# Fused attention and mixture of experts on one core: SyncE's queue in the source's order, weight quarters held for a GpSimd write, and a gather that the weights wait for

## The chip, the cores and the metric

One core of one Trainium2 chip runs the whole program in one launch. The metric is device microseconds of that core, the median of the runs. TensorE (PE) multiplies; VectorE (DVE), ScalarE (ACT) and GpSimd (POOL) do the elementwise work; SyncE (SP) issues nearly all the DMAs.

## The reference

The first half is attention with eight global keys and a causal window of 96, on (4 batches, 8 heads, 768 positions, 64 wide):

```python
keep = is_global | is_local
scores = np.where(keep, scale * q @ k.T - slopes * dist, -1e9)
a = exp(scores - max); a = a / (a.sum(-1) + 1e-9)
x = (a @ v)                       # 3072 tokens of 512
```

The second half routes each token to the best of 8 experts by `x @ w_gate`. An expert keeps its 80 tokens of the largest gate value and computes `gate * (relu(x @ w1[e]) @ w2[e])`, with w1[e] 512 by 1024 and w2[e] 1024 by 512. All other rows of the (3072, 512) output are zero.

## The kernel before

All data are fp32. **Attention** goes through 24 blocks of 128 positions in the order TURN, in two rounds of four heads each, so that round u treats block u // 2 (`for u in range(nu - 1)`, L344, with the last round written out in DRAIN). A round is a pipeline over engines: PE makes the scores of round u (L156), DVE adds the position table and takes the minimum (L167), ACT takes the exponential (L171), GpSimd divides by the sum for round u - 1 (`norm`, L184), PE transposes the probabilities of round u - 2 (L201 to L214), ACT and DVE copy them to SBUF (L218, L224), and PE multiplies those of round u - 3 by the values (`weigh`, L246, L256). Every fourth round also computes router logits. The first compare of DVE (L167) marks where a round stands.

Blocks are loaded into four buffers each of q, va and vb (`load_blk`, L383, called in even rounds for the block two ahead, that is four rounds ahead). The keys of the next batch come in three pieces (`keys`, L348). The first 16 of 64 **weight quarters** of 512 KB are loaded during attention (`ahead`, L350), and the whole output is cleared by twelve DMAs of zeros of 512 KB (`wipe`, L352). PE, DVE, ACT and GpSimd run in the order of the source (`manual_schedule(engines=ORDERED)`); SyncE is not among them, so a planner chooses the order in which the DMAs stand in its queue.

Attention's result is kept transposed. It must lie in DRAM by rows (`x_dram`) for a later gather. For 8 of the 24 blocks (INSIDE) the turning back is done within the rounds from 29 (FROM) on, beside the probabilities' transposes (L214), half a block per round, and stored from the same copy (L227). Three more blocks are turned in the drain (`x`, `y`, L101 to L107), and 13 in `select` (`rows`, L109 to L122): PE transposes two blocks, ACT copies them to one of three pairs of buffers, SyncE stores them. ROWS gives how many such pairs stand at each step of the search.

**The drain** (DRAIN, L52) is a hand-written order of steps; `r` is one step of the routing of a group of blocks, `c` one of the last group's choice, `x` the turning of a block. **`select`** searches the gate value at which each expert has 80 tokens, then compares ranks with slot numbers (`at`, L688, four compares of 480 elements) and multiplies (L692) to get the index table `gi`. **`experts`** gathers each expert's 80 rows by an indirect DMA on GpSimd's queue (`gather`, L724), fills PE's wait with idle products (`busy`, 11 and 7 of them, L542), transposes the first expert's tokens (`tokens`, L756) and then runs both layers of each expert as three fp32r products per tile (L762), with the weights split into two parts by ACT (L740) and DVE (L743, a few on GpSimd). A split frees the buffer for the next of the remaining 48 quarters (L85).

Of the kernel before, what the change touches and what calls it, by code (L numbers as in the profile page):

```python
# [10 lines left out]
F32 = mybir.dt.float32  # L11
# [11 lines left out]
P = 128  # L23
# [21 lines left out]
MASK = -8.0e9 * 64  # L45

EARLY = "k12 q1 v0 k23 v1 q2 k36 w0 v2"
WIPE = 34
FROM, INSIDE = 29, 8


DRAIN = (  # L52
    "r a1 t45 w44 r r r n47 r r a2 t46 r r r r w45 r r r "
    "t47 w46 r b1 w47 r r b2 c1 c c2 c r r x x x c3 y y y r r c c r"
)
NORM = (("V", slice(2, 4)), ("G", slice(0, 2)))
ROWS = (2, 2, 1, 0, 2)
WARM = (0, 0, 0, 0, 0, 11)
SPLIT = (4, 4, 4)
FAR = 1.0e6  # L60
# [4 lines left out]
def fast_path(tc, a, out, cst, x_dram, inp):  # L65
# [4 lines left out]
    with ExitStack() as ctx:  # L70
# [7 lines left out]

        def load_w():

            for k, e, c in QUARTERS:
                t = wp.tile([P, DF], F32, tag="w", name=f"w{k}_{e}_{c}")
                raw[k, e, c] = t
                src = (a["w1"] if k == 1 else a["w2"])[e].rearrange("(c p) f -> p c f", p=P)
                yield nc.sync.dma_start(out=t.rearrange("p (c f) -> p c f", c=k), in_=src[:, k * c:k * c + k])  # L85

# [5 lines left out]
                )  # L92

        room = inp.kt[1].rearrange("p q k -> p (q k)")[:, :6 * DM].rearrange("p (n d) -> p n d", n=6)
        due = [INSIDE]
        halves = [slice(64 * i, 64 * i + 64) for i in range(2)]

        def turned(t, xp):
# [10 lines left out]
        def rows(t, n, xp):  # L109

            xp = xp.rearrange("p i (n c) -> p i n c", n=2)
            for j in range(n):
                ut = uts.pop(t + j)
                for pr in range(NP):
                    for i, h in enumerate(halves):
                        T.transpose(out=xp[:, i, j, 64 * pr:64 * pr + 64], in_=ut[h, pr, :], identity=ident[h, h])
            j = 2 * (t // 2 % 3)
            x = room[:, j:j + n].rearrange("p n (i c) -> p n i c", i=2)
            A.copy(out=x, in_=xp[:, :, :n].rearrange("p i n c -> p n i c"))
            for j in range(n):  # L120
                nc.sync.dma_start(
                    out=x_dram[TURN[t + j] * P:(TURN[t + j] + 1) * P, :], in_=x[:, j].rearrange("p i c -> p (i c)"))  # L122

        with tc.tile_pool(name="at_sb", bufs=2) as sp, tc.tile_pool(name="ps_a", bufs=1, space=PSUM) as psa, ExitStack() as pctx:
# [215 lines left out]
            weights = load_w()  # L340
            ahead = islice(weights, NW)
            wipe = clear()
            sp_ctx.enter_context(tc.manual_schedule(engines=ORDERED))
            for u in range(nu - 1):  # L344
                if u % (2 * NB) == 1 and u // 2 // NB + 1 < B:
                    keys = inp.keys(u // 2 // NB + 1)
                if keys and u % 2 == 0:
                    keys = keys if next(keys, END) is not END else None  # L348
                elif u > 1:
                    next(ahead, None)  # L350
                if u >= WIPE:
                    next(wipe, None)  # L352
                if u == 0:
                    next(cst["first"])
                begin(u)
                scores(u)
                if u % 4 == 0 and 8 <= u:
                    logits2(u // 2 - 4, 2)
                if u == 0:
                    window = window_tables(nc, cst)  # L360
                if 2 <= u:
                    copied(u - 2)
                if u == 0:
                    for _ in cst["first"]:
                        pass
                if u < 2:
                    for _ in islice(window, 3 - u):
                        pass
                if u == 1:
                    for z in pwz:  # L370
                        G.memset(z[:, 4 * WH:], 0.0)
                    G.memset(cst["zero"], 0.0)
                if u == 2:
                    for _ in window:
                        pass
                if u > 2:
                    for _ in range(3):
                        next(late, None)
                if u % 4 == 3 and 7 <= u:
                    logits1((u - 7) // 2, 2)  # L380
                if 3 <= u:
                    weigh(u - 3)
                if u % 2 == 0 and 3 <= u // 2 + 2 < NT:  # L383
                    inp.load_blk(u // 2 + 2)
                routes(3)
            u = nu - 1
            begin(u)
# [272 lines left out]
def select(tc, cst, lps, gs1, rows, due, w, early):  # L660

    nc = tc.nc
    V, G, T = nc.vector, nc.gpsimd, nc.tensor
    gi, si, gs, bx = cst["gi"], cst["si"], cst["gs"], cst["bx"]

    with tc.tile_pool(name="sel2", bufs=2) as s2, tc.tile_pool(name="ps_s", bufs=1, space=PSUM) as pp, \
            tc.tile_pool(name="ps_r", bufs=2, space=PSUM) as pr, tc.manual_schedule(engines=ORDERED):
        slot = s2.tile([P, NT], BF16, name="slot", bufs=1)

        def more(n):  # L670
            for _ in range(min(n, (NT - due[0] + 1) // 2)):
                t = due[0]
                due[0] = min(NT, t + 2)
                rows(t, due[0] - t, pr.tile([P, 2, 512], F32, tag="xp", name=f"xp{t}"))

        for i, own in enumerate(search(nc, s2, s2, pp, cst, gs1, slot)):
            if i == len(ROWS):
                break
            more(ROWS[i])
            for j in range(len(early)):  # L680
                if SPLIT[j] == i:
                    nc.scalar.copy(out=early[j], in_=w[1, 0, j])
            busy(nc, cst, lps, WARM[i])
        more(NT)
        ix = pp.tile([CAP, 6, E], F32, tag="cnt", name="ix")
        for i in range(4):
            at = s2.tile([P, CAP, NT // 4], BF16, tag="at", bufs=4, name=f"at{i}")
            V.tensor_tensor(  # L688
                out=at, in0=cst["svx"], in1=slot[:, 6 * i:6 * i + 6].unsqueeze(1).broadcast_to([P, CAP, 6]), op=ALU.is_equal)
            for j in range(6):  # L690
                t = 6 * i + j
                T.matmul(ix.rearrange("p k e -> p (k e)"), at[:, :, j], bx[:, t].rearrange("p k e -> p (k e)"), start=t == 0, stop=t == NT - 1)  # L692
        busy(nc, cst, lps, WARM[-1])
        with nc.allow_low_precision(reason="integers"):
            V.tensor_reduce(out=gi, in_=ix[:, :2, :].rearrange("p k e -> p e k"), axis=AX.X, op=ALU.add)
        xs = s2.tile([CAP, 6, E], F32, name="xsel")
        V.tensor_copy(out=xs, in_=ix)
        tok = s2.tile([CAP, E], F32, name="tok")
        V.tensor_tensor(out=tok, in0=xs[:, 0, :], in1=xs[:, 1, :], op=ALU.add)
        V.tensor_tensor(out=gs, in0=xs[:, 3, :], in1=xs[:, 4, :], op=ALU.add)  # L700
        V.tensor_tensor(out=gs, in0=gs, in1=xs[:, 5, :], op=ALU.add)
        vm = s2.tile([CAP, E], F32, name="vm")
        V.tensor_scalar(out=vm, in0=xs[:, 2, :], scalar1=-BIG, scalar2=BIG, op0=ALU.mult, op1=ALU.add)
        V.tensor_tensor(out=si, in0=tok, in1=vm, op=ALU.add)
        full = s2.tile([1, E], F32, name="full")
        V.tensor_tensor(out=full, in0=own, in1=cst["cap8"][:1], op=ALU.is_equal)
        V.tensor_reduce(out=cst["sure"], in_=full, axis=AX.X, op=ALU.min)


def experts(tc, out, cst, x_dram, inp, raw, weights, lps, early, hip):  # L710
# [5 lines left out]
    with tc.tile_pool(name="ffn", bufs=2) as fp, tc.tile_pool(name="hl", bufs=NLO) as hl, \  # L716
# [97 lines left out]
                ready[k, e, c] = split(raw.pop((k, e, c)), DF, f"w{k}_{e}_{c}")  # L814
                next(weights, None)

        with tc.manual_schedule(engines=ORDERED):
            for e in range(E):
                gather(e)
            prepare(2)  # L820
            busy(nc, cst, lps, 7)
            tokens(0)
            prepare(2)
            for e in range(E + 1):
# [277 lines left out]
def late_constants(nc, a, c, fast=True):  # L1102
# [37 lines left out]
    yield iota(nc, sv, 1, 1)  # L1140
    yield iota(nc, s1, 2, 1)
    yield V.scalar_tensor_tensor(out=s1, in0=sv, scalar=cap, in1=s1, op0=ALU.is_le, op1=ALU.mult)
    yield V.tensor_scalar(out=c["svx"], in0=s1.unsqueeze(2).broadcast_to([P, CAP, NT // 4]), scalar1=-1.0, scalar2=None, op0=ALU.add)


def late_tiles(c):
    for n, k in (("pref", E), ("kval", 31), ("kval1", P - 1), ("tval", NT), ("pval", E), ("cap8", E), ("capm", E), ("pick", E), ("gate", NT)):
        c.tile(n, [P, k])
    for n, k in (("sval", CAP), ("sval1", CAP), ("ones", P), ("ones32", P), ("ones16", P), ("tri", P), ("keep", 2 * E * (NT + 1)), ("mz", 2 * E * (NT + 1))):
        c.tile(n, [P, k], BF16)  # L1150
    c.tile("svx", [P, CAP, NT // 4], BF16)
    c.tile("bx", [P, NT, 6, E], BF16)
    c.tile("gs1", [P, E], BF16)
    c.tile("left", [P, 2, NT])
# [13 lines left out]
class Inputs:  # L1168
# [4 lines left out]
    def __init__(self, nc, a, ip):  # L1173
        self.nc, self.a, self.ip = nc, a, ip
        self.kts, self.blk = {}, {}
        self.q = [ip.tile([P, NP * P], F32, name=f"q{i}") for i in range(self.NQ)]
        self.kt = [ip.tile([P, NP, NB * KB], F32, name=f"kt{i}") for i in range(2)]
        self.va, self.vb = ([ip.tile([P, H * D], F32, name=f"{n}{i}") for i in range(self.NQ)] for n in ("va", "vb"))
        for g in range(2):
            self.load_k(0, slice(2 * g, 2 * g + 2), 0, KB)  # L1180
            self.load_q(0, slice(2 * g * P, 2 * g * P + 2 * P))
# [113 lines left out]
```

## Time and profile before

| | us |
|---|---|
| median of 3 runs | 282.01 |
| lowest and highest | 280.45, 283.68 |
| the profiled execution | 283.87 |
| its span, first to last instruction | 282.2 |
| mean granted TensorE clock, share of full | 0.94 |

The profiled execution lies 1.9 us above the median; 1.7 us of its time lie outside the span. Times in the rows count from the start of the span. Attention takes the span up to about 150 us, the drain and `select` up to 171, the gather up to 179, the experts up to 278, and the last scatter the rest. A row of a timeline gives the start, the duration of the merged instructions, engine, line, what is written from what, and their number; in brackets the idle time of the engine before it and what ended it.

### The profile page before, as it was taken

How to read it: one execution, taken by the hardware profiler on the slowest of the kernel's cores; microseconds unless marked ns; L12 is line 12 of the kernel's file. 1: busy time of each engine (PE TensorE's matmuls, PEld its weight loads, DVE VectorE, ACT ScalarE, POOL GpSimd, SP SyncE). 2: the span in 40 equal slices, each digit the busy share in tenths (PEclk: the TensorE clock that was granted, in tenths of full speed). 3: DMA queues.
4: the chain of work that ended last, by engine and by line, in shares of the span. 5: the costliest groups of instructions: out<-in, count | busy, mean ns of one | idle time of the engine just before them, and what ended most of it. 6: DMA issues, size and time to landing. Idle time of an engine off the chain costs nothing. (4 is left out here: it accounts for less than half of the span.)

```text
span 282.2 us, 9562 instructions
## 1 busy us (share of the span) xinstructions
PE 254.0 (90%) x3565; PEld 185.8 (66%) x3565; DVE 216.4 (77%) x784; ACT 206.1 (73%) x582; POOL 123.9 (44%) x171
## 2 busy tenths in 40 slices
PE   2699799969899999999999799699999999999992
PEld 2477577657667778778776685366666666656661
DVE  3967557766757898688977675579999999998960
ACT  2778667965748888898886554478798977979740
POOL 5356543533326534653544403750717346152421
PEclk9999979997959999999999857799999999999997
DMA  6999999999999996564210485999999999992001
GB/s 181 307 282 384 300 314 340 325 299 317 331 397 358 388 372 215 160 211 156 94 42 20 147 313 193 259 319 362 313 300 390 380 343 394 339 354 79 23 28 29
DMA packets 40875, 73.06 MB, mean 259 GB/s; under 512 B 3413, under 2 KB 14549, under 8 KB 40821
## 3 DMA queue, kind: packets, MB, share of 16 engines
q1 hardware_dynamic: 39652, 69.74, 73.8%
q0 software_dynamic: 1024, 2.62, 3.2%
q8 instruction: 30, 0.49, 0.8%
q14 instruction: 25, 0.20, 0.2%
q10 hardware_dynamic: 144, 0.00, 0.0%
HBM read 58.46 MB, written 13.89 MB: 256 GB/s over the span
## 5 line engine op out<-in xcount | busy, mean ns | idle before, releaser
L171 ACT ACTIVATE pwz<-ts,nm 128x168 f32<-128x168 f32 (+1 forms) x192 | 80.8, 422 | 34.3 <-DVE nm L167 32.9
L184 POOL TENSOR_TENSOR pwz<-pwz,z 128x672 f32<-128x672 f32 (+2 forms) x48 | 60.4, 1257 | 75.3 <-ACT pwz L171 66.2
L167 DVE CUSTOM_DVE_ANT_0 ts<-sc,tab 128x168 f32<-128x168 f32 (+1 forms) x192 | 53.2, 315 | 30.0 <-PE sc L156 29.7
L156 PE MATMUL sc<-kt,q 64*64 64x104 f32 (+3 forms) x1088 | 45.8, 290 | 11.8 <-issue 6.0
L156 PEld LDWEIGHTS sc<-kt,q 64*64 64x64 f32 x1088 | 36.1, 146 | 14.6 <-issue 13.6
L743 POOL TENSOR_TENSOR w_3l<-w,w_3h 128x1024 fp32r<-128x1024 f32 x7 | 23.7, 3382 | 43.9 <-issue 26.3
L171 ACT ACTIVATION_READ_ACCUMULATOR pwz<-ts,nm 128x1 f32 x192 | 36.2, 188 | 0.0
L246 PE MATMUL u<-ta,va 104*64 104x128 f32 (+1 forms) x384 | 33.6, 299 | 0.4 <-ACT kt L271 0.4
L743 DVE TENSOR_TENSOR w_0l<-w,w_0h 128x1024 fp32r<-128x1024 f32 x15 | 28.3, 1890 | 3.0 <-ACT w_0h L740 3.0
L256 PE MATMUL u<-ta,vb 64*64 64x64 f32 x640 | 28.6, 231 | 0.0
L256 PEld LDWEIGHTS u<-ta,vb 64*64 64x64 f32 x640 | 22.9, 140 | 7.3 <-issue 6.3
L201 PE MATMUL tp<-ident,pwz 64*128 64x64 f32 x384 | 23.9, 246 | 4.2 <-POOL pwz L184 3.4
L246 PEld LDWEIGHTS u<-ta,va 104*64 104x64 f32 (+1 forms) x384 | 21.2, 143 | 9.7 <-issue 6.1
L224 DVE COPY ta<-tp 128x384 f32<-128x384 f32 (+2 forms) x48 | 27.5, 574 | 0.0
L201 PEld LDWEIGHTS tp<-ident,pwz 64*128 64x128 f32 x384 | 16.9, 147 | 12.4 <-POOL pwz L184 7.4
L218 ACT COPY ta<-tp 128x384 f32<-128x384 f32 (+2 forms) x48 | 22.8, 475 | 0.8 <-ACT pwz L171 0.8
L743 DVE TENSOR_TENSOR w_2l<-w,w_2h 128x1024 fp32r<-128x1024 f32 x15 | 19.8, 1320 | 0.5 <-ACT w_2h L740 0.5
L805 POOL DMA_INDIRECT out_dram<-vb,si x8 | 12.7, 1590 | 12.9 <-ACT vb L804 12.0
L743 DVE TENSOR_TENSOR w_1l<-w,w_1h 128x1024 fp32r<-128x1024 f32 x15 | 18.2, 1211 | 0.0
L740 ACT CAST w_2h<-w 128x1024 fp32r<-128x1024 f32 x15 | 15.9, 1058 | 1.2 <-PE hp L762 1.2
L740 ACT CAST w_3h<-w 128x1024 fp32r<-128x1024 f32 x16 | 16.7, 1046 | 0.0
L740 ACT CAST w_1h<-w 128x1024 fp32r<-128x1024 f32 x15 | 15.7, 1050 | 0.5 <-PE hp L762 0.5
(405 smaller groups left out, 519.7 us busy)
## 6 DMA issues: line engine op xcount, KB each, us to landing
w<-in_w_dram SPq DMA_DIRECT2D x64, 512.0 KB
out_dram<-zero SPq DMA_DIRECT2D x12, 512.0 KB
q<-in_q_dram SPq DMA_DIRECT2D x23, 256.0 KB
vb<-in_vb_dram SPq DMA_DIRECT2D x20, 256.0 KB
va<-in_va_dram SPq DMA_DIRECT2D x20, 208.0 KB
x_dram<-kt SPq DMA_DIRECT2D x13, 256.0 KB
kt<-in_kT_dram SPq DMA_DIRECT2D x4, 816.0 KB
x_dram<-ta SPq DMA_DIRECT2D x16, 128.0 KB
```

Source lines behind the costliest of these rows:

```text
L156: T.matmul(sc[64 * i:64 * i + 64, hh, pp, o:o + e - c], q[h, pr * P + 64 * i:pr * P + 64 * i + 64], kt[h, pr, c0 + c:c0 + e], start=True, ...
L167: V.tensor_tensor_reduce(out=ts[:, j, :w], in0=sc[:, hh, pp, :w], in1=cst["tab" if m else "tab0"][:, 2 * g + pp, hh, :], scale=-0.125, sca ...
L171: A.activation(out=pw[:, j, :w], in_=ts[:, j, :w], func=AF.Exp, bias=nm[:, j:j + 1], scale=-1.0, accum_out=z[:, j:j + 1],)
L184: eng.tensor_tensor(out=p, in0=p, in1=zs.unsqueeze(2).broadcast_to(list(p.shape)), op=ALU.mult)
L201: T.transpose(out=tps[i][:, 64 * j:64 * j + 64], in_=pw[hs[i], o:o + P], identity=ident[hs[i], hs[i]])
L218: A.copy(out=ta[:, 0, :n], in_=tps[0][:, :n])
L224: V.tensor_copy(out=ta[:, 1, :n], in_=tp[:, :n])
L246: T.matmul(up[64 * hh:64 * hh + 64, pr, :], va[:n, 64 * h:64 * h + 64], ta[:n, :, 64 * j:64 * j + 64], start=pp == 0 and (g == 0 or last), ...
L256: T.matmul(up[h, pr, 64 * i:64 * i + 64], vb[h, i, pr, :], ta[h, i, 256 + 64 * pp:320 + 64 * pp], start=False, stop=True, skip_group_check ...
L740: A.copy(out=hi, in_=src)
L743: eng.tensor_tensor(out=lo, in0=src, in1=hi, op=ALU.subtract)
L805: G.indirect_dma_start(out=out[:, :], out_offset=bass.IndirectOffsetOnAxis(ap=si[:, e:e + 1], axis=0), in_=y, in_offset=None, bounds_check ...
```

## The change

SyncE's queue joins the engines that keep the source's order, in attention and in `experts`. A quarter of weights is loaded at the end of each odd round from 3 to 33; before it, GpSimd writes one element of its tile, which the DMA must wait for. The clearing DMAs go to rounds 6, 10, ... 30 and 36, 38, ... 44. Ten blocks instead of eight are turned inside attention, from round 26 on; eleven instead of thirteen remain for `select`, in five pairs of buffers instead of three (the two new ones are buffers of va, which become one tile), and only one, of a single block, is left for the step after the ranks. In the drain one more `r` comes before the three `x`. Three of the four compares write `at` with the slots contiguous, from a new constant `svt`. A two-element DMA that reads the first gather's rows is put into SyncE's queue behind the gathers and before the next weights, and the `busy` products there are 5 instead of 7.

```diff
-WIPE = 34
-FROM, INSIDE = 29, 8
+WIPE = (*range(6, 31, 4), *range(36, 45, 2))
+FROM, INSIDE = 26, 10
 DRAIN = (
...
-    "t47 w46 r b1 w47 r r b2 c1 c c2 c r r x x x c3 y y y r r c c r"
+    "t47 w46 r b1 w47 r r b2 c1 c c2 c r r r x x x c3 y y y r r c c r"
 )
-ROWS = (2, 2, 1, 0, 2)
+ROWS = (2, 2, 1, 0, 1)
...
+                if n < NW:
+                    G.memset(t[:1, :1], 0.0)
...
-            j = 2 * (t // 2 % 3)
-            x = room[:, j:j + n].rearrange("p n (i c) -> p n i c", i=2)
+            j = 2 * ((t - due[1]) // 2 % 5)
+            x = (room[:, j:j + n] if j < 6 else inp.v4[:, j - 6:j - 6 + n]).rearrange("p n (i c) -> p n i c", i=2)
...
-            sp_ctx.enter_context(tc.manual_schedule(engines=ORDERED))
+            sp_ctx.enter_context(tc.manual_schedule(engines=ORDERED | {ET.SP}))
...
-                elif u > 1:
-                    next(ahead, None)
-                if u >= WIPE:
+                if u in WIPE:
                     next(wipe, None)
...
+                if u % 2 and u > 2:
+                    next(ahead, None)
                 routes(3)
...
+            ts = slot[:, 6 * i:6 * i + 6]
+            if i:
+                at = s2.tile([P, NT // 4, CAP], BF16, tag="at", bufs=3, name=f"at{i}")
+                V.tensor_tensor(out=at, in0=cst["svt"], in1=ts.unsqueeze(2).broadcast_to([P, 6, CAP]), op=ALU.is_equal)
+            else:
+                at = s2.tile([P, CAP, NT // 4], BF16, name="at0", bufs=1)
+                V.tensor_tensor(out=at, in0=cst["svx"], in1=ts.unsqueeze(1).broadcast_to([P, CAP, 6]), op=ALU.is_equal)
+                at = at.rearrange("p s t -> p t s")
...
-        with tc.manual_schedule(engines=ORDERED):
+        with tc.manual_schedule(engines=ORDERED | {ET.SP}):
             for e in range(E):
                 gather(e)
+            nc.sync.dma_start(out=cst["scl"][:1], in_=xgs[0][:1, :2])
             prepare(2)
-            busy(nc, cst, lps, 7)
+            busy(nc, cst, lps, 5)
...
-        self.va, self.vb = ([ip.tile([P, H * D], F32, name=f"{n}{i}") for i in range(self.NQ)] for n in ("va", "vb"))
+        self.v4 = ip.tile([P, self.NQ, H * D], F32, name="va")
+        self.va = [self.v4[:, i] for i in range(self.NQ)]
+        self.vb = [ip.tile([P, H * D], F32, name=f"vb{i}") for i in range(self.NQ)]
```

## Rows read from the trace of the kernel before

**Rows 1.** Busy time by stretch, cut at DVE's first compare of rounds 4 and 28, 12 and 16, 31 and 47. The columns are the stretch and its length, then PE, weight load, DVE, ACT and POOL busy time (instructions), the granted clock as a share of full, the DMA engines' busy share, and GB/s.

```profile
16.84:93.94 77.10, 69.84 (x1397) 53.73 (x1399) 51.05 (x304) 56.42 (x229) 35.95 (x54) 0.91 1.04 336
43.30:53.33 10.03, 9.64 (x222) 7.42 (x224) 7.14 (x48) 8.99 (x38) 4.70 (x4) 1.00 1.06 332
101.73:147.36 45.63, 44.88 (x1060) 35.66 (x1054) 37.94 (x211) 39.17 (x152) 22.50 (x24) 1.00 0.52 168
```

**Rows 2.** Timeline of PE, the three longest pauses within attention; "issue" means that no releaser is shown.

```profile
35.43 0.54 PE L156 MATMUL sc<-kt,q 64*64 64x104 f32 x13 [2.26 <-issue]
...
62.95 0.54 PE L156 MATMUL sc<-kt,q 64*64 64x104 f32 x13 [2.32 <-issue]
...
77.30 0.53 PE L156 MATMUL sc<-kt,q 64*64 64x168 f32 x11 [1.14 <-issue]
```

**Rows 3.** Busy time by stretch, the columns as in rows 1, for the stretches of attention that ran at the lower clock.

```profile
36.80:40.20 3.40, 3.40 (x58) 2.79 (x54) 1.74 (x11) 2.53 (x11) 1.91 (x4) 0.50 1.04 310
64.10:67.50 3.40, 3.40 (x43) 2.20 (x37) 1.75 (x11) 2.05 (x9) 1.31 (x1) 0.50 1.04 358
77.80:84.50 6.70, 6.70 (x82) 4.42 (x76) 3.77 (x25) 3.05 (x14) 1.63 (x2) 0.50 1.06 398
```

**Rows 4.** The list of DMA issues: what, count, KB each.

```profile
w<-in_w_dram SPq DMA_DIRECT2D x64, 512.0 KB
out_dram<-zero SPq DMA_DIRECT2D x12, 512.0 KB
q<-in_q_dram SPq DMA_DIRECT2D x23, 256.0 KB
vb<-in_vb_dram SPq DMA_DIRECT2D x20, 256.0 KB
va<-in_va_dram SPq DMA_DIRECT2D x20, 208.0 KB
...
kt<-in_kT_dram SPq DMA_DIRECT2D x4, 816.0 KB
...
kt<-in_kT_dram SPq DMA_DIRECT2D x3, 544.0 KB
kt<-in_kT_dram SPq DMA_DIRECT2D x5, 272.0 KB
```

**Rows 5.** Timeline of SyncE's queue: the first and the last quarter of weights before the experts, and the first clearing DMA.

```profile
12.52 0.34 SPq L85 DMA_DIRECT2D w<-in_w_dram  x1
...
64.58 0.33 SPq L85 DMA_DIRECT2D w<-in_w_dram  x1
...
70.16 0.62 SPq L89 DMA_DIRECT2D out_dram<-zero  x1
```

**Rows 6.** Timeline of GpSimd, a small write in round 1.

```profile
10.74 0.23 POOL L371 MEMSET pwz<- 128x24 f32 x3
```

**Rows 7.** Timelines of PE and DVE in the drain.

```profile
155.57 1.51 PE L101 MATMUL xp<-ident,ut 128*128 128x128 f32 x12
156.91 0.34 PE L549 MATMUL lps<-oh,cf 128*127 128x8 bf16 x4
...
157.30 0.16 DVE L490 TENSOR_TENSOR capm<-capm,lps 127x8 f32<-127x8 f32 x1 [1.34 <-PE lps L549]
```

**Rows 8.** Timelines of DVE and PE from the drain's compares to the end of `select`.

```profile
153.09 0.75 DVE L499 TENSOR_TENSOR cf<-sx,kval 128x254 bf16<-128x254 f32 x2
...
167.88 1.37 DVE L688 TENSOR_TENSOR at<-svx,slot 128x480 bf16<-128x480 bf16 x4
171.25 0.17 DVE L695 TENSOR_REDUCE gi<-ix 80x8 int32<-80x16 f32 x1 [2.00 <-PE ix L692]
...
166.73 1.54 PE L116 MATMUL xp<-ident,kt 64*128 64x64 f32 x24
168.35 2.87 PE L692 MATMUL ix<-bx,at 128*80 128x48 bf16 x24
171.04 4.93 PE L542 MATMUL lps<-svx,ones 128*128 128x480 bf16 x18
```

**Rows 9.** The gathers: GpSimd's instructions of line 724 (durations in ns, min/median/max) with the time from issue to landing, then the first gather, PE's wait for it, and the weights in SyncE's queue behind the stores.

```profile
L724 POOLq EVENT_SEMAPHORE  x5: 17/43/1374, 169.6 to 172.8; - x5
...
DMA to landing us min/median/max: 4.4/5.5/7.9
...
173.81 1.22 POOL L724 DMA_INDIRECT q<-x_dram,gi  x1 [11.15 <-issue]
...
178.31 0.47 PE L756 MATMUL xf<-ident,q 80*128 80x80 f32 x4 [2.34 <-DMA q<-x_dram,gi]
...
173.90 77.30 SPq L85 DMA_DIRECT2D w<-in_w_dram  x48
```

**Rows 10.** PE's first products of the experts on its timeline, and the stretch at the lower clock (columns as in rows 1).

```profile
180.13 0.59 PE L762 MATMUL hp<-early,xt0h 128*80 128x512 f32 x1
...
183.50 0.43 PE L762 MATMUL hp<-early,xt0l 128*80 128x512 f32 x1
...
184.29 0.39 PE L762 MATMUL hp<-w_2l,xt0h 128*80 128x512 f32 x1
...
185.20 0.39 PE L762 MATMUL hp<-early,xt0l 128*80 128x512 f32 x1
...
180.20:183.50 3.30, 3.30 (x9) 1.89 (x8) 3.30 (x4) 1.98 (x2) 2.80 (x2) 0.50 0.94 229
```

More of the change, by code (lines that the diff above doesn't have):

```diff
@@ L79, in load_w @@
         def load_w():
-            for k, e, c in QUARTERS:
+            for n, (k, e, c) in enumerate(QUARTERS):
                 t = wp.tile([P, DF], F32, tag="w", name=f"w{k}_{e}_{c}")
                 raw[k, e, c] = t
+                if n < NW:
+                    G.memset(t[:1, :1], 0.0)
                 src = (a["w1"] if k == 1 else a["w2"])[e].rearrange("(c p) f -> p c f", p=P)
@@ L94, in fast_path @@
         room = inp.kt[1].rearrange("p q k -> p (q k)")[:, :6 * DM].rearrange("p (n d) -> p n d", n=6)
-        due = [INSIDE]
+        due = [INSIDE, INSIDE + 3]
         halves = [slice(64 * i, 64 * i + 64) for i in range(2)]
@@ L686, in select @@
         for i in range(4):
-            at = s2.tile([P, CAP, NT // 4], BF16, tag="at", bufs=4, name=f"at{i}")
-            V.tensor_tensor(
-                out=at, in0=cst["svx"], in1=slot[:, 6 * i:6 * i + 6].unsqueeze(1).broadcast_to([P, CAP, 6]), op=ALU.is_equal)
+            ts = slot[:, 6 * i:6 * i + 6]
[6 more added lines that the diff above has]
+                at = at.rearrange("p s t -> p t s")
             for j in range(6):
                 t = 6 * i + j
-                T.matmul(ix.rearrange("p k e -> p (k e)"), at[:, :, j], bx[:, t].rearrange("p k e -> p (k e)"), start=t == 0, stop=t == NT - 1)
+                T.matmul(ix.rearrange("p k e -> p (k e)"), at[:, j], bx[:, t].rearrange("p k e -> p (k e)"), start=t == 0, stop=t == NT - 1)
         busy(nc, cst, lps, WARM[-1])
@@ L1142, in late_constants @@
     yield V.scalar_tensor_tensor(out=s1, in0=sv, scalar=cap, in1=s1, op0=ALU.is_le, op1=ALU.mult)
+    yield V.tensor_scalar(out=c["svt"], in0=s1.unsqueeze(1).broadcast_to([P, NT // 4, CAP]), scalar1=-1.0, scalar2=None, op0=ALU.add)
     yield V.tensor_scalar(out=c["svx"], in0=s1.unsqueeze(2).broadcast_to([P, CAP, NT // 4]), scalar1=-1.0, scalar2=None, op0=ALU.add)
@@ L1151, in late_tiles @@
     c.tile("svx", [P, CAP, NT // 4], BF16)
+    c.tile("svt", [P, NT // 4, CAP], BF16)
     c.tile("bx", [P, NT, 6, E], BF16)
```

## The prediction

> **What bounds the kernel now.** I read the time by stretch first. From round 4 to round 28 attention took 77.10 us for 24 rounds, with the DMA engines' share at 1.04 and 336 GB/s [rows 1]. Rounds 12 to 15 took 10.03 us, 2.51 each, at full clock and without a pause, and at that pace 24 rounds take 60.2 us. So 16.9 us of this stretch are not work. From round 31 on, where the DMA share is 0.52, 16 rounds took 45.63 us, 2.85 each, with the turning of finished blocks inside [rows 1]. Next I read what PE waits for: three pauses of 2.26, 2.32 and 1.14 us in the midst of the scores, with no releaser named [rows 2]. All three lie in the full-DMA stretch, none from round 31 on. The low-clock stretches begin inside or right behind them, at 1.2 GHz by the granted 0.50 [rows 3]: 13.5 us in which PE started 58 + 43 + 82 = 183 products, where rounds 12 to 15 started 222 in 10.03 us, 299 in 13.5 us. That costs 116 / 22.1 per us = 5.2 us. Pauses and clock together are 5.72 + 5.2 = 10.9 us of the 16.9. What PE lacks in the pauses is not shown; I infer something fetched by a DMA, since they come only while the DMA engines are full.
>
> They are full because the planner issues early: all 16 quarters by 64.6 us and then zeros from 70.2 us [rows 5], though the source puts zeros into rounds from 34 on. The end of the kernel is bound otherwise: the experts keep PE busy throughout, and this change doesn't touch that work.
>
> **The change part by part.** Attention, rounds 4 to 27. The new order issues in them 12 quarters and 6 zeros of 512 KB, 12 q of 256, ten va and vb pairs of 464 and two v of 256 (counted as a vb), and the keys' pieces 544 + 816 + 272 + 544 + 816 + 272 [rows 4]: 20,700 KB, 21.2 MB. At 336 GB/s that takes 63.1 us, where 77.10 x 336 GB/s = 25.9 MB went before. So the gain lies between 0 (the engines stay full, the pauses stay) and 77.1 - 63.1 = 14.0 us (the DMA's own time). I take 8.2, three quarters of the 10.9 of pauses and clock: the demand then is 21.2 MB in 68.9 us, 308 GB/s, nearer to the full rows than to the 168 GB/s from round 31 on, so I leave a pause in. A page of the Trainium skill, "DMA: Bandwidth & Descriptors" (Specifications), puts the HBM limit of a core at about 358 GB/s; by it the transfers would take an estimated 59.2 us, less than PE's 60.2, and the gain would be 16.9. The stretch as a whole held 336 [rows 1], a part of it 398 [rows 3], so the figure is neither reached for long nor a ceiling in this trace.
>
> The write that holds a quarter: 16 small GpSimd writes, three of which took 0.23 us together [rows 6], some 1.2 us in all on an engine that is busy 36 of 77 us [rows 1]. Cost nothing; cover gone, 1.2 us. But SyncE now stands still until GpSimd has passed the division of its round, and behind it wait the next keys, zeros and block. PE, which needs that block four rounds later, is the one that would wait (third rival).
>
> Turning two more blocks inside: four more half-blocks, so four rounds at 2.85 instead of 2.51 [rows 1], +1.4 us. The two pairs that fall out of `select` save little there: PE's 24 transposes before the index products become 8, 1.0 us at the 1.54 of [rows 8], but the products wait for `slot` until 167.9 anyway. Their worth is in the stores, below. `svt` is one more DVE operation of a size that takes about 0.34 us [rows 8], in a stretch where DVE is busy 51 of 77 us: nothing, or 0.4. The later zeros, 2.6 MB, fall where the DMA share is 0.52: nothing.
>
> Drain. The third `r` puts the count (0.34 us) ahead of the 12 transposes, which take 1.51 us and for which DVE waits 1.34 [rows 7]. That wait goes; next late is the last group's count behind the same transposes. Between 0 and 1.3 I take half, -0.7.
>
> The compares. Three of four now repeat the slot along the inner dimension. The nearest rows for that are 0.375 us per 254 elements, so about 0.54 to 0.6 for 480 against 0.34 now [rows 8]. The last is then ready at about 169.9; PE, at 2.87 / 24 = 0.12 per product, reaches the last six at 168.35 + 18 x 0.12 = 170.5. So it is hidden, and the weight columns are as many as before: 0. If the compare takes twice that, +1.
>
> Stores and gather. GpSimd waits up to 1.37 us, until 172.8, for the last store, and starts the first gather 1.0 later [rows 9]; `gi` is there at 171.42 [rows 8]. With one block instead of three after the ranks, the last store is issued about 1.5 to 2 us earlier, before `gi`: -1.4. The gather took 4.4 us to land, beside the weights issued at 173.90 [rows 9]. Held behind it, they leave between 0 and the 2 us or so that separate 4.4 from the wait of 2.34; I take 1.0, the lower half, because its own issue (1.2 us) stays. That makes -2.4, but PE's idle products must also be done: two fewer at the later rate, 18 in 4.93 us, end near 175.5. The first transposes come at 178.31 - 2.3; I count -2.3. The held weights cost nothing: the last of the 48 is issued at 251.2 [rows 9], some 26 us before the end of the products, so 2 us later is covered; without that cover, +2.
>
> Clock behind it. PE idles 2.34 us [rows 9], then ran at 1.2 GHz until 183.5: 8 products from 180.13 to 183.50 at 0.42 us against 0.23 (184.29 to 185.20, four steps) [rows 10]. With the gap closed this is 8 x 0.19 = -1.6.
>
> Sum: -8.2 + 1.4 - 0.7 - 2.3 - 1.6 = -11.4. The profiled execution took 283.9 (span 282.2 and 1.7 around it), which gives 272.5; the median lies 1.9 below it, so 270.6 against 282.0. I write 270.5.
>
> **Rivals.** First: the paced queue is enough, the pauses all vanish. The 20,700 KB spread evenly and the later rounds without a pause speak for it. Then -14.0 + 1.4 - 4.6 = -17.2, 264.8.
>
> Second: the DMA engines stay as full as now, or the pauses have another cause, and PE pauses as before. For it: 21.2 MB in 60.2 us, PE's own pace, is 352 GB/s, above the 336 now. Then 1.4 - 4.6 = -3.2, 278.8. This is also the result if the hold does nothing because GpSimd runs ahead. The same page (Queues, rings and completion order) says that DMA engines alternate between queues packet by packet. By that rule something on another queue waits for a packet, not for the backlog, so the pauses would not shrink with it, and the 1.0 of the held weights would go too: 279.8. The trace shows a gather landing in 4.4 to 7.9 us with weights under way [rows 9] and cannot separate the two.
>
> Third, slower: the blocks come late. Before, SyncE ran ahead; now a q is issued four rounds, 10.0 us, before use, and in rounds 6 and 18 behind a quarter, a zero and 816 KB of keys, 1.9 MB or 5.6 us at 336 GB/s, on top of what is still under way. If a pair of rounds pauses 1.1 us (the least pause with the low clock near it [rows 2, 3]) and loses 1.3 us at 1.2 GHz (5.2 us over four such stretches of 3.4), it costs 2.4. Eleven such pairs: 60.2 + 26.4 = 86.6 us against 77.1, so +9.5 + 1.4 - 4.6 = +6.3, 288.3. It decides from nine pairs on (16.9 + 3.2 = 20.1; 20.1 / 2.4 = 8.4). Against it: 5.6 us plus landing is inside 10.0.
>
> **How the numbers follow.** My forecast gets 0.47, within 267 to 274; the first rival 0.25, the second 0.20, the third 0.08. The predicted time is the forecast's. Leaving out the third rival and the ends of the first two, the range is 263 to 279.5. About 1% (2.8 us) is what a measurement here tells from no change, so faster means under 279.2: forecast and first rival, and half of the second, 0.82; within 1% 0.10; slower 0.08.
>
> **What would show it.** DVE's first compares of rounds 4 and 28 should lie 63 to 71 us apart (77.10 before), with at most one pause of PE over 1 us and at most 5 us of low clock between them. PE's transposes in the drain should follow the count. GpSimd should start the first gather within 1.2 us of `gi`, and PE should go from idle products to the first transposes with under 1 us between, and stay at full clock. I am wrong if the three pauses are still there, if PE waits for a q or va by name, or if SyncE's queue is seen waiting for GpSimd while PE waits for a block.

## The result and the profile after

The changed kernel took 272.68 us (median of 4 runs, 271.79 to 273.44) beside 282.85 of the kernel before on the same chip: a ratio of 0.967, 95% interval 0.961 to 0.974. A second set of 6 runs gave 272.59 (270.39 to 273.25), the kernel before in it 282.79. The medians here take all executions of a kernel; the ratios and their intervals leave out those more than 1.5% above its fastest. The profiled execution took 272.45, its span 270.6 against 282.2. The forecast was 270.5, its range 263 to 279.5.

First the busy time by stretch, cut at DVE's first compare (now L169) of rounds 4 and 28, of 12 and 16, of 31 and 47, with the columns of [rows 1]:

```profile
16.71:83.92 67.21, 63.24 (x1397) 49.11 (x1399) 51.61 (x305) 56.04 (x229) 36.39 (x67) 1.00 0.97 310
39.90:49.92 10.02, 9.48 (x214) 7.14 (x212) 7.73 (x50) 8.96 (x38) 4.75 (x6) 1.00 0.96 291
91.94:139.66 47.72, 45.61 (x1060) 36.00 (x1054) 37.91 (x212) 39.40 (x153) 22.55 (x26) 1.00 0.85 277
```

Rounds 4 to 27 took 9.9 us less (77.10 in [rows 1]; 9.3 less in the second set's profile, 67.80) at full clock throughout. The DMA share went from 1.04 to 0.97 there and from 0.52 to 0.85 in the last row: the loads moved to where room was, and that row is 2.1 us longer than in [rows 1]. Rounds 12 to 15 are what they were.

PE's pauses over 0.4 us in attention from round 4 on, from its timeline, where [rows 2] had 2.26, 2.32 and 1.14:

```profile
33.17 0.87 PE L158 MATMUL sc<-kt,q 64*64 64x104 f32 x24 [0.71 <-DMA q<-in_q_dram]
...
65.86 0.87 PE L158 MATMUL sc<-kt,q 64*64 64x104 f32 x24 [0.45 <-DMA q<-in_q_dram]
70.28 0.80 PE L158 MATMUL sc<-kt,q 64*64 64x168 f32 x17 [0.95 <-issue]
101.76 0.87 PE L158 MATMUL sc<-kt,q 64*64 64x104 f32 x24 [0.84 <-DMA q<-in_q_dram]
...
106.19 0.21 PE L211 MATMUL tp<-ident,pwz 64*128 64x64 f32 x1 [0.49 <-issue]
```

None is over 1 us, and three of five now name a q: the blocks do come late, as the third rival said, but for 2.0 us in all. The first two belong to the blocks whose q is issued in rounds 6 and 18, the rounds that this rival named; SyncE issued them at 24.69 and 56.49, and PE went on at 33.17 and 65.86, 8.5 and 9.4 us later. The second set's profile has a longer wait for the first of them:

```profile
33.51 0.87 PE L158 MATMUL sc<-kt,q 64*64 64x104 f32 x24 [1.51 <-DMA q<-in_q_dram]
```

Next the drain and `select`, timelines of PE and DVE, to lay beside [rows 7, 8]:

```profile
148.07 0.34 PE L551 MATMUL lps<-oh,cf 128*127 128x8 bf16 x4
148.27 1.51 PE L103 MATMUL xp<-ident,ut 128*128 128x128 f32 x12
149.61 0.23 PE L551 MATMUL lps<-oh,cf 128*127 128x8 bf16 x2
150.55 0.17 PE L616 MATMUL jb<-gs,ones 128*128 128x8 bf16 x1 [0.71 <-ACT q L108]
...
159.50 2.30 PE L699 MATMUL ix<-bx,at 128*80 128x48 bf16 x24 [0.93 <-DVE at L695]
161.63 5.63 PE L544 MATMUL lps<-svx,ones 128*128 128x480 bf16 x16
167.69 0.47 PE L763 MATMUL xf<-ident,q 80*128 80x80 f32 x4 [0.43 <-DMA q<-x_dram,gi]
```

```profile
159.04 0.41 DVE L695 TENSOR_TENSOR at<-svx,slot 128x480 bf16<-128x480 bf16 x1
159.37 1.79 DVE L692 TENSOR_TENSOR at<-svt,slot 128x480 bf16<-128x480 bf16 x3
161.84 0.17 DVE L702 TENSOR_REDUCE gi<-ix 80x8 int32<-80x16 f32 x1 [0.69 <-PE ix L699]
```

The count stands ahead of the 12 transposes. The index products took 2.30 instead of 2.87, and their wait is now DVE's compare. PE waits 0.43 for the gather, not 2.34 [rows 9].

The gather, in GpSimd's instructions of its line and on the timelines of GpSimd and SyncE:

```profile
L731 POOLq EVENT_SEMAPHORE  x5: 17/43/3757, 158.4 to 162.9; - x5
...
DMA to landing us min/median/max: 3.0/6.2/9.3
```

```profile
163.91 1.64 POOL L731 DMA_INDIRECT q<-x_dram,gi  x1 [10.27 <-DVE sure L714]
```

```profile
159.28 0.40 SPq L123 DMA_DIRECT2D x_dram<-kt  x1
...
168.44 70.43 SPq L87 DMA_DIRECT2D w<-in_w_dram  x48
```

The wait of 3757 ns ended at 162.7; `gi` was done at 162.01, and the last store, issued at 159.28, is what came last: by the trace's semaphore updates 15 of its 16 parts had landed by 161.74, the sixteenth at 162.69. (The releaser in brackets, `sure`, ran at 162.98, after that wait; the gather starts 1.0 to 1.2 behind the end of this wait in the kernels of both sides.) Last, the stretches around the gather, columns as above:

```profile
155.92:166.16 10.24, 9.09 (x64) 5.49 (x64) 7.94 (x21) 4.69 (x6) 1.94 (x2) 0.50 0.50 186
166.20:169.50 3.30, 2.36 (x13) 1.07 (x11) 0.84 (x2) 1.30 (x3) 2.53 (x3) 1.00 0.51 143
```

The low-clock stretch of `select` ended before the experts began; the one behind the gather [rows 10] is gone.

By stage, from the first compares, `jb`, `gi`, the first gather and transposes, after less before: rounds 4 to 27 -9.9; rounds 28 to 46 +2.3; round 47 to `jb` -0.6; `jb` to `gi` -1.1; `gi` to the gather -0.5; its landing to the first transposes -0.7; the clock behind it -1.5; the other experts +0.6. Sum -11.4, of 11.5.

### The profile page after: what moved, and what is told of

Read it like the earlier page. It is cut to its first block, busy times and chain, and to the rows that moved or that the text cites. A ratio compares the mean times of both kernels' runs of the same rounds, so it can differ in the third digit from the quotient of the medians.

```text
span 270.6 us, 9583 instructions
## 1 busy us (share of the span) xinstructions
PE 245.7 (91%) x3563; PEld 178.9 (66%) x3563; DVE 214.4 (79%) x785; ACT 205.3 (76%) x581; POOL 121.1 (45%) x187
## 5 line engine op out<-in xcount | busy, mean ns | idle before, releaser
L173 ACT ACTIVATE pwz<-ts,nm 128x168 f32<-128x168 f32 (+1 forms) x192 | 80.8, 423 | 26.4 <-DVE nm L169 24.9
L186 POOL TENSOR_TENSOR pwz<-pwz,z 128x672 f32<-128x672 f32 (+2 forms) x48 | 60.3, 1257 | 67.2 <-ACT pwz L173 58.1
L169 DVE CUSTOM_DVE_ANT_0 ts<-sc,tab 128x168 f32<-128x168 f32 (+1 forms) x192 | 53.2, 314 | 22.4 <-PE sc L158 22.0
L158 PE MATMUL sc<-kt,q 64*64 64x104 f32 (+3 forms) x1088 | 42.5, 283 | 9.1 <-DVE kt L1065 5.3
L158 PEld LDWEIGHTS sc<-kt,q 64*64 64x64 f32 x1088 | 33.7, 142 | 11.5 <-issue 7.7
L750 POOL TENSOR_TENSOR w_3l<-w,w_3h 128x1024 fp32r<-128x1024 f32 x7 | 19.9, 2845 | 45.1 <-issue 28.3
L248 PE MATMUL u<-ta,va 104*64 104x128 f32 (+1 forms) x384 | 32.9, 291 | 0.7 <-ACT kt L273 0.4
L750 DVE TENSOR_TENSOR w_0l<-w,w_0h 128x1024 fp32r<-128x1024 f32 x15 | 24.9, 1661 | 6.5 <-ACT w_0h L747 6.5
L258 PE MATMUL u<-ta,vb 64*64 64x64 f32 x640 | 27.4, 224 | 0.0
L258 PEld LDWEIGHTS u<-ta,vb 64*64 64x64 f32 x640 | 21.9, 134 | 6.9 <-issue 6.5
L203 PEld LDWEIGHTS tp<-ident,pwz 64*128 64x128 f32 x384 | 16.5, 142 | 11.6 <-POOL pwz L186 7.4
L169 DVE DVE_READ_ACCUMULATOR2_ANT nm<- 128x1 f32 x192 | 15.8, 82 | 0.0
```

The lines of the kernel that those rows point to most:

```text
L158: T.matmul(sc[64 * i:64 * i + 64, hh, pp, o:o + e - c], q[h, pr * P + 64 * i:pr * P + 64 * i + 64], kt[h, pr, c0 + c:c0 + e], start=True, ...
L169: V.tensor_tensor_reduce(out=ts[:, j, :w], in0=sc[:, hh, pp, :w], in1=cst["tab" if m else "tab0"][:, 2 * g + pp, hh, :], scale=-0.125, sca ...
L173: A.activation(out=pw[:, j, :w], in_=ts[:, j, :w], func=AF.Exp, bias=nm[:, j:j + 1], scale=-1.0, accum_out=z[:, j:j + 1],)
L186: eng.tensor_tensor(out=p, in0=p, in1=zs.unsqueeze(2).broadcast_to(list(p.shape)), op=ALU.mult)
L203: T.transpose(out=tps[i][:, 64 * j:64 * j + 64], in_=pw[hs[i], o:o + P], identity=ident[hs[i], hs[i]])
L248: T.matmul(up[64 * hh:64 * hh + 64, pr, :], va[:n, 64 * h:64 * h + 64], ta[:n, :, 64 * j:64 * j + 64], start=pp == 0 and (g == 0 or last), ...
```

## The experiments

**The two parts that pace the queue, taken out singly and together.**

```diff
 a_nohold:
-                if n < NW:
-                    G.memset(t[:1, :1], 0.0)
 a_planned:
-            sp_ctx.enter_context(tc.manual_schedule(engines=ORDERED | {ET.SP}))
+            sp_ctx.enter_context(tc.manual_schedule(engines=ORDERED))
 a_neither: both
```

> The changed kernel without the one-element GpSimd write that holds each quarter; nothing else. Theory (the hold is what spreads the loads: without it SyncE issues a quarter as soon as its buffer is free, all 16 early, and the DMA engines are full as before): rounds 4 to 28 take 70 to 77 us instead of 67.2, with pauses of PE over 1 us and some low clock back, and the time is 275 to 282. Rival (SyncE's order of the source is enough, since a quarter then stands behind the blocks and keys of its round, which wait for their own buffers): rounds 4 to 28 at 66 to 69 us, no pause over 1 us, time 272 to 274.

> The changed kernel with SyncE's order in attention left to the planner again; the hold and the rounds of the zeros stay in the source. Theory (order and hold are both needed: the planner puts zeros and quarters where it likes): rounds 4 to 28 at 72 to 77 us, time 276 to 283. Rival (the hold alone paces the queue, because a quarter that waits for GpSimd keeps all that stands behind it): rounds 4 to 28 at 66 to 69 us, time 272 to 274.

> The changed kernel with neither the hold nor SyncE's order in attention; the zeros' rounds and the place of the quarters in the source stay as changed. Without the hold alone rounds 4 to 28 took 70.2 us, without the order alone 71.0, with both 67.2. Theory (each of the two keeps the planner or the queue from issuing early, and either does most of the work): without both, rounds 4 to 28 are back at 75 to 78 us with two or more pauses of PE over 1 us, time 279 to 283. Rival (the two add up and the rest comes from the zeros' and quarters' places in the source): 73 to 74.5 us (67.2 + 3.0 + 3.8), time 276 to 278.5.

Medians: 273.64 without the hold, 275.83 without the order, 278.47 without both (10 runs, 275.22 to 281.85), 272.6 with both. The ratios to the kernel before on the same chip are 0.966 (95% interval 0.960 to 0.973), 0.976 (0.967 to 0.984), 0.987 (0.981 to 0.993), and 0.967 (0.961 to 0.974) with both. Rounds 4 to 28 of each, in that order, as stretches:

```profile
16.68:86.83 70.15, 64.08 (x1397) 49.38 (x1399) 51.57 (x306) 55.95 (x229) 35.97 (x54) 1.00 0.96 311
```

```profile
16.72:87.72 71.00, 64.44 (x1397) 49.86 (x1399) 51.95 (x306) 56.27 (x229) 36.43 (x67) 1.00 1.05 360
```

```profile
16.83:87.03 70.20, 64.18 (x1397) 49.38 (x1399) 51.95 (x305) 55.92 (x229) 35.90 (x54) 1.00 1.04 355
```

The source's order is what empties the engines (360 and 355 GB/s without it, 311 with it); the hold alone doesn't. Only the loss without both is clear of the noise: 5.9 us of median. The order's 3 is likely, and the hold's 1 isn't shown, since the ratio without it is that of the changed kernel. Its profile, of its slowest execution, has the 70 us of its theory, but the DMA share of its rival: the share of a whole stretch doesn't set the pauses alone. My theory for the last run (75 us or more) fell, and so did its rival's 73 to 74.5, although the median lies within the rival's 276 to 278.5: with the DMA engines as full as before, this execution still took 70.2. Its longest pause without a releaser was 1.17, with no low clock behind it, and rounds 28 to 46 took 57.4, 2.25 of them in one wait for ACT. So a full queue makes long pauses possible; how long they are, and whether the clock falls behind one, differs between executions, and one profile doesn't show what the median of ten runs lost.

**What the pauses are.** Small products that nothing reads, ahead of round 2 in the kernel before, 16 in the source:

```diff
 b_shift:
+                if u == 2:
+                    for _ in range(16):
+                        T.matmul(lps[:32, :32], ident[:, :32], ident[:, :32], start=True, stop=True, skip_group_check=True)
                 begin(u)
                 scores(u)
```

> The kernel before with 16 small products that nothing reads put ahead of the scores of round 2; its results are the same. Theory (PE's long pauses stand at fixed distances in PE's own stream of instructions: it lacks its next instructions, whose fetch is late while the DMA engines are full): the three pauses come at the same counts of PE's products as before, 469, 973 and 1226 within a few, so 16 products earlier in the program, about a third of a round. Rival (PE lacks data, a q or a key): the pauses stay at the same place of the program, ahead of the same scores, so at counts 485, 989 and 1242.

One run, 279.75 us. PE's timeline at its pauses (two more without a releaser, of 0.94 and 0.53, are left out):

```profile
34.00 0.49 PE L246 MATMUL u<-ta,va 104*64 104x128 f32 x5 [1.26 <-issue]
...
41.48 0.65 PE L246 MATMUL u<-ta,va 104*64 104x128 f32 x6 [1.55 <-issue]
...
61.79 0.49 PE L246 MATMUL u<-ta,va 104*64 104x128 f32 x5 [0.64 <-issue]
...
75.28 0.44 PE L246 MATMUL u<-ta,va 104*64 104x128 f32 x3 [1.05 <-issue]
```

They left the scores (L156 in [rows 2]) for another product, and counted along PE's timeline they stand at products 469, 596, 973 and 1226. Three are the counts of the kernel before to the product; the fourth is one step of 127 beyond 469, and a pause of 0.94 at 1100 lies on the same steps. The trace shows the 16 products as 32 on PE (L357), so the rival's places were 501, 1005 and 1258, not the 485, 989 and 1242 that I had written; no pause is at either. On the same grid lie the pauses of other kernels here: 343, 469, 1100, 1226, 1603 and 1856 without the hold; 469, 973, 1226, 1352 and 1478 without the order; 1226 and 1982 in the changed kernel, where PE's other three waits, at 458, 1153 and 1883, name a q. So a pause without a releaser belongs to PE's own instruction stream, and not to any data.

There is one possible place per 126 products or so; counted with their weight loads and with PE's semaphore instructions, which the trace records too, the places stand 256 entries apart, within one (961, 1985 and 2498 for the three pauses of the kernel before). The page of every kernel here has this row, with 0.7% or 0.8%:

```profile
q8 instruction: 30, 0.49, 0.8%
```

30 packets of 0.49 MB are 16 KB each, and the 7,241 entries of PE's stream in the changed kernel over 256 are 28.3. The trace's DMA records hold the time of each packet, and they tie the pauses to them: in all 46 pauses without a releaser over 0.4 us in the attention of these 14 profiles, PE goes on 1.3 to 1.7 us behind the end of one such packet (1.52, 1.44 and 1.29 for [rows 2]). In the kernel before the next packet starts 2.5 to 5.3 us after PE has passed a place in rounds 4 to 27, at a DMA share of 1.04, and 0.1 to 2.4 us after it from round 31 on, at 0.52. So PE lacks its next instructions, and their packets start later where the DMA engines are full. Why they start later, no run shows. The Trainium skill, "Runtime: NRT & Kernel Launch" (Instruction fetch mechanics), says that an engine's instructions are fetched in 16 KiB blocks of 256 by a DMA queue of its own, and calls the cost of a block's edge mostly hidden. The size agrees with the 256 entries counted here; "mostly hidden" holds where the queue is light, and at 1.04 of DMA share an edge cost up to 2.3 us.

**All clearing DMAs late.**

```diff
 a_late:
-WIPE = (*range(6, 31, 4), *range(36, 45, 2))
+WIPE = (*range(34, 46),)
 a_late_rows, besides:
-ROWS = (2, 2, 1, 0, 1)
+ROWS = (2, 2, 1, 1, 0)
```

> The changed kernel with all twelve clearing DMAs in rounds 34 to 45, so that six of them (3.1 MB of some 21) leave rounds 4 to 28. Theory (what is left of PE's loss there still goes with the DMA engines' load): rounds 4 to 28 take 62.5 to 65 us instead of 67.2, the rounds from 28 to 47 lose no more than 1 of it, time 268.5 to 271. Rival (what is left is the pipeline's own, waits between PE, DVE, ACT and GpSimd that no load sets): rounds 4 to 28 at 66.5 to 67.5, the later rounds 0 to 1 us longer, time 272.5 to 273.7.

270.06 us (269.62 to 270.64), 65.3 us for rounds 4 to 28 at a DMA share of 0.88, and 54.9 for the rest although the share there rose to 0.99:

```profile
16.88:82.20 65.32, 62.30 (x1397) 48.29 (x1399) 51.56 (x305) 55.83 (x229) 36.37 (x67) 1.00 0.88 281
82.20:137.11 54.91, 53.20 (x1238) 42.36 (x1237) 45.84 (x254) 46.57 (x181) 26.53 (x30) 1.00 0.99 333
```

One pause without releaser is left in rounds 4 to 28, 0.62 at product 469. In this profile the theory holds, a little short of its size.

> The kernel with all zeros from round 34 on, and the last single block turned one step of the search earlier (2, 2, 1, 1, 0), so that nothing is stored after the ranks. Theory (the first gather waits for the last store, 0.5 us beyond the index table): GpSimd starts the first gather 1.2 to 1.4 us behind the table's end instead of 1.7, time 0.3 to 0.6 below that with the zeros alone (270.06): 269.3 to 269.9. Rival (PE's and ACT's turn stands in the search's way one step earlier, or the landing eats it): 270 to 271.

> The changed kernel itself, word for word, beside the kernel with the zeros from round 34 on and an earlier last store, so that the two are compared on one chip: 272 to 273.5. If the late zeros bring what the run without the earlier store showed (270.06), the other is 2 to 4 us below it.

270.75 us (6 runs, 269.11 to 273.24) beside 272.59 for the changed kernel on the same chip. The gather came earlier as expected, 1.14 behind the start of `gi` instead of 2.07 (1.65 in the changed kernel's second profile), and PE didn't wait for it at all:

```profile
163.81 0.17 DVE L702 TENSOR_REDUCE gi<-ix 80x8 int32<-80x16 f32 x1 [0.69 <-PE ix L699]
```

```profile
164.95 1.21 POOL L731 DMA_INDIRECT q<-x_dram,gi  x1 [10.22 <-DVE full L713]
```

The median didn't follow: the profiled execution, the slowest of the six, lost more in attention, 1.71 us in one pause at product 469 and 3.4 us of low clock behind it, 68.5 us for rounds 4 to 28. Over both comparisons the late zeros are 1.8 to 2.6 us below the changed kernel, but their ratios to the kernel before, 0.963 (0.957 to 0.969) and 0.964 (0.955 to 0.973), overlap the changed kernel's 0.967 and 0.969 (0.960 to 0.977). So their gain is likely and not shown, and the earlier store on top is unproven.

**Attention's part alone, on the kernel before:** the zeros' rounds, the quarter at the end of odd rounds, the hold and SyncE's order in attention, and nothing else of the diff.

```diff
 b_attn, on the kernel before:
-WIPE = 34
+WIPE = (*range(6, 31, 4), *range(36, 45, 2))
...
+                if n < NW:
+                    G.memset(t[:1, :1], 0.0)
...
-            sp_ctx.enter_context(tc.manual_schedule(engines=ORDERED))
+            sp_ctx.enter_context(tc.manual_schedule(engines=ORDERED | {ET.SP}))
...
+                if u % 2 and u > 2:
+                    next(ahead, None)
                 routes(3)
```

> The kernel before with the attention's part of the change alone: SyncE in the source's order in attention, the zeros' rounds, a quarter at the end of odd rounds, the hold. Theory (attention gives 8.2 to 9.9 of the 11.4): rounds 4 to 28 at 66.5 to 68 us instead of 77.1, all stages behind it as before, time 272.5 to 274.5. Rival (part of the gain in those rounds belongs to the other parts, or a shorter attention is given back in the drain by late stores): 275 to 279.

274.79 us (273.06 to 278.19) against 281.92, so about 7 of the 10 us by the medians; the ratio, 0.983 with an interval of 0.972 to 0.994, would allow anything from 2 to 8. Rounds 4 to 28 took 66.0. With eight blocks inside, rounds 28 to 46 still took 55.75. The other parts together bring the rest, 2 to 3 by the medians.

**Eight blocks inside, three after the ranks.**

```diff
 a_in8:
-FROM, INSIDE = 26, 10
+FROM, INSIDE = 29, 8
-ROWS = (2, 2, 1, 0, 1)
+ROWS = (2, 2, 1, 0, 2)
 a_in8_busy, besides:
-            busy(nc, cst, lps, 5)
+            busy(nc, cst, lps, 9)
```

> The changed kernel with eight blocks turned inside attention from round 29 on, as before the change, and three blocks after the ranks in place of one. Theory (my prediction's terms: four inside-rounds cost 1.4 us, and the early stores save 1.4 before the gather): rounds 28 to 47 take 1.4 us less than the 55.7 of the changed kernel, the last store is issued after the index table and the first gather starts 2.2 to 3 us behind it instead of 2.07, time 272 to 273. Rival (the inside turns cost more than they save, since rounds 28 to 47 came out 2.3 us longer in the changed kernel): rounds 28 to 47 at 53.4, gather 2.1 to 2.6 behind the table, time 270.5 to 271.8.

> The changed kernel with eight blocks turned inside and three after the ranks, as in the run before that came out at 276.3 while its profiled execution took 272.5, and with 9 idle products behind the index products instead of 5. Theory (the later gather leaves PE idle for 2.3 us, and in most executions the clock falls behind that gap): with the gap filled the median is 272 to 273.5 and the granted clock at 0.97 or more in all executions. Rival (the slow executions lose their time elsewhere): 275 to 277 again.

The first gave 276.31 (272.54 to 277.73), outside both expectations; its profiled execution was its fastest, with rounds 28 to 46 at 55.0, the gather 2.99 behind `gi`, and PE idle before the first transposes:

```profile
168.17 0.47 PE L763 MATMUL xf<-ident,q 80*128 80x80 f32 x4 [2.31 <-DMA q<-x_dram,gi]
```

Yet the clock stayed at full behind this gap:

```profile
168.17:171.60 3.43, 2.91 (x14) 1.79 (x15) 2.46 (x3) 2.92 (x4) 2.82 (x3) 1.00 0.62 170
```

With four more idle products the median was 273.17 (270.82 to 273.82), granted clock 0.969 to 0.985 where the first had 0.962 to 0.973 in its slower runs. That would fit a clock that falls behind the gap in other executions, but no profile of a slower one was taken, so the place of its loss stays open. By the medians two more blocks inside are worth 3.7 us (272.6 against 276.3; the ratio is 0.986, 0.978 to 0.995), and filling the gap gets within 0.6 of them. That they are worth it because they close this gap is not shown.

**The weights that wait for the gather, and the compares' layout.**

```diff
 a_noscl:
-            nc.sync.dma_start(out=cst["scl"][:1], in_=xgs[0][:1, :2])
 a_strided:
-            if i:
+            if False:
...
-                at = s2.tile([P, CAP, NT // 4], BF16, name="at0", bufs=1)
+                at = s2.tile([P, CAP, NT // 4], BF16, tag="at", bufs=4, name=f"at{i}")
```

> The changed kernel without the two-element DMA that makes the weights wait for the first gather. Theory (the weights issued beside the gather slow its landing): gather to first transposes 4.4 to 4.6 us instead of 3.8, PE waits 1.1 to 1.3 us instead of 0.4; if the clock then falls behind the gap as it did before, 1.5 more: 273.4 to 275. Rival (the gather's landing is its own latency, the shorter one in the changed kernel comes from elsewhere): landing 3.8 us, time 272.5 to 272.9.

274.33 us. The gather took 5.5 us from issue to PE's transposes instead of 3.8, PE waited 1.46, and the low clock was back behind it (stretch, columns as before):

```profile
167.85 0.47 PE L763 MATMUL xf<-ident,q 80*128 80x80 f32 x4 [1.46 <-DMA q<-x_dram,gi]
```

```profile
169.00:172.40 3.40, 3.40 (x9) 1.95 (x9) 3.40 (x4) 2.47 (x3) 2.79 (x3) 0.50 0.89 217
```

This pair lies near the ends of two ranges: from the gather's start to the transposes it is 3.7 to 4.3 us in the ten profiles with held weights, and 4.5 to 5.5 in the four without, 0.9 more on average. So the theory holds, at half the size that this pair shows.

> The changed kernel with all four compares in the old, strided form. Theory (the contiguous layout makes PE load its columns faster, 0.067 us per index product instead of 0.11): the index products take about 0.11 us each, and from the slots to the index table 3.3 to 3.5 us instead of 2.84, time 273.0 to 273.5. Rival (my prediction's step: the layout is worth nothing, and the table came earlier because of the clock alone): slots to table 2.8 to 3.0 us, time 272.5 to 272.8.

272.33 us. The index products took 2.87 again, as in [rows 8], at the same low clock, and `gi` came 3.36 behind the first compare instead of 2.80:

```profile
159.72 2.87 PE L699 MATMUL ix<-bx,at 128*80 128x48 bf16 x24 [0.93 <-DVE at L695]
```

But the first gather started 4.85 behind the first compare, beside 4.87 in the changed kernel: the last store's wait took all of the 0.56. The layout does what the theory says, and the time doesn't show it.

## Why the prediction held, step by step

**The sum, right by luck in part.** The profiled executions differ by 11.4, as forecast, but from terms that miss in both directions: attention and the compares gave 1.7 and 1.1 more, the gather's two terms together 1.1 less, and rounds 28 to 46 and the experts cost 0.9 and 0.6 more than I had counted. The median came out 2.2 above the forecast: I took off the 1.9 by which the profiled execution of the kernel before lay above its median, and that of the changed kernel lies 0.2 below its own.

**Attention, right in mechanism, 1.7 short in size.** I took -8.2, leaving a pause in; -9.9 came (-9.3 in a second profile). The three things that its test named were there: 67.2 us, no pause over 1 us without a releaser, no low clock. But one of my signs of being wrong was there too: PE waits for a q by name, up to 0.84, and 1.51 in the second profile. It cost 2.0 us and not the third rival's 26.4. "Something fetched by a DMA" was the right guess, and the shift of the products shows whose: PE's instruction stream. I credited the pacing as one thing; the runs show the two parts' joint worth, likely 3 us for the order alone, and nothing sure for the hold alone.

**Rivals.** The first, a queue so even that all pauses vanish, didn't come, and late zeros go half the way to it. The second named packet-by-packet alternation, by which pauses would not shrink with the backlog: in this case they did, and the gather beside the weights took 0.9 us longer on average, so sharing costs there. The limit of 358 GB/s that the prediction cites from the Trainium skill didn't bound the stretch either: 360 were held over 71 us. The third showed in kind, 2.0 us of waits for q, in the rounds that it named: I had set 5.6 us plus landing against the 10.0, and PE got its block 8.5 and 9.4 us after the issue.

**Two more blocks inside, mis-sized.** I took +1.4 from four rounds at 2.85; the stretch grew by 2.3. With the loads moved there but eight blocks inside it took 54.0, 55.0 and 55.75 in three kernels; with ten inside and the same attention, 54.05 to 55.9 in four profiles. So the blocks' own cost doesn't stand out from that spread, and the moved loads, such as the q with its 0.84 at 101.76, are the likelier source of most of the growth from 53.4. "The later zeros fall where the DMA share is 0.52: nothing" missed that quarters and q move there too.

**Drain, right:** -0.6 for -0.7. What is late next was not the last count but the turn's copy, PE's 0.71 for ACT's L108.

**Compares, wrong step, no harm.** "The weight columns are as many as before: 0" failed: with contiguous columns a product took 0.07 us instead of 0.11 at the same clock, and DVE, with 0.6 per compare as I said, set the pace. `gi` gained 0.56 by it; the rest of the 1.1 goes by argument to the clock, which was low for 11.6 us between `jb` and `gi` before, 5.9 after, and 8.9 in the second profile, which gained 0.7.

**Stores and gather, the step that failed.** I took -1.4 for the store wait, because the last store is issued before `gi`. It was, 2.56 before, and still landed last: 3.45 us from issue to the end of the wait, where the kernel before had 2.5 (issued at 170.29, the end in [rows 9]). 0.95 of this is the one late part of its sixteen; in the kernel before the last part came 0.04 behind the others. Only -0.5 came (-0.9 in the second profile, where the store took 3.0). Issued one search step earlier, it freed the gather, 1.14 behind `gi`. The held weights, 0.9 over all profiles, were close to my 1.0; -0.7 shows here. "The held weights cost nothing" holds only nearly. The last quarter is issued at 238.9, earlier than before. But PE takes 11.6 us from the 61st to the 81st of the experts' `hp` products in all ten profiles with held weights, and 11.0 in the four without, and only in the ten it waits for a split weight there:

```profile
190.62 0.46 PE L769 MATMUL hp<-w_2l,xt2h 128*80 128x512 f32 x1 [0.34 <-DVE w_2l L750]
```

By the last of these products 0.2 to 0.3 of the 0.6 is left: it starts 85.0 us behind the first transposes in the changed kernel, 84.7 and 84.8 behind them in the two profiles with neither held weights nor low clock there.

**Clock behind the gather, right in size, its cause not shown:** -1.5 for -1.6. Without the held weights low clock and gap were back. But six profiles have a gap of 1.0 to 2.3 us there and full clock behind it, one of them that of the kernel before with the shifted products (1.13). So a closed gap goes with full clock in every profile, a gap goes with either, and what else decides stays open: that -1.5 came in this pair of profiles is luck in part.

## What to carry to other kernels

A pause of PE without a releaser while DMA engines are full may be its own instruction fetch: look for a fixed pitch in the count of its instructions (256 here), and shift the program by a few to test it. Bulk loads that nothing needs soon belong in the stretch with the lowest DMA share, in a written order; a further write that holds them was not shown to bring more. A store is out of the way when it has landed, not when it is issued: price it by issue to the landing of its last part.

## What had not been expected

PE's pauses without a releaser fall on one grid of 256 instructions, some 126 products with their loads, in all kernels here, whatever the instruction is. A DMA share of 0.99 with 333 GB/s in rounds 28 to 46 cost those rounds nothing (54.9 against 55.7 in the changed kernel), while 1.05 with 360 GB/s in rounds 4 to 28 went with 71.0 us, where 0.88 went with 65.3. And weights read with contiguous columns loaded faster at the same clock: 24 products, 18 of them so, in 2.30 us, still waiting for DVE, instead of 2.87.
